# Staggered tracing of projection, MLP and key sums, and LN scaling on ACT, in a kernel of two attention and two MLP layers

## The chip, the cores and the metric

The kernel runs on one core of one Trainium2 chip. The metric is the device time of one execution in microseconds (us), given as the median of several executions. The profiles are single executions. A span is about 2 us shorter than the device time of the same execution (525.43 against 523.7 us for the kernel before). Of the runs e1 to e4 below, a second profile is kept beside the one quoted; between the two, one stretch of the kernel differs by up to 2.7 us. So a difference of one or two us between single profiles is not read as an effect here.

Engine names: PE is TensorE's matmul stream, PEld its weight loads, DVE VectorE, ACT ScalarE, POOL GpSimd, SP the engine that issues most DMAs here. LN is the layer normalization of a tile of rows. The granted clock is the share of TensorE's full clock that it was allowed in a stretch of time.

## The reference, cut to what matters

```python
def _A_ref(x, wqkv, w_phi, wo):          # linear attention, 32 heads of 16
    q, k, v = ...                        # x @ wqkv, split by head
    pq, pk = q @ w_phi, k @ w_phi        # per head
    phi_q = concat(softmax(pq), softmax(-pq))
    phi_k = concat(softmax(pk), softmax(-pk))
    kv = sum over s of phi_k^T v;  z = sum over s of phi_k
    o = (phi_q kv) / (phi_q z + 1e-6)
    return o @ wo

def _B_ref(x, W_gate, W_up, W_down):     # MLP, 512 -> 1376 -> 512
    return (relu(x @ W_gate) * (x @ W_up)) @ W_down

x = x + A(layernorm(x));  x = x + B(layernorm(x))     # x is 2048 x 512, bf16
x = x + A(layernorm(x));  x = x + B(layernorm(x))     # the same weights again
```

An attention layer needs the sums kv and z over all 2048 rows before it can answer the first query. That is a hard joint: all keys of a layer come before its first attention tile. An MLP needs only its own rows.

## The kernel before

The rows are cut into 4 chunks of 512, a chunk into 4 tiles of 128. The residual X stays in SBUF. The query and key weights are folded with `w_phi` once, at the start. LN of a tile makes statistics on DVE, the inverse root on POOL, the scaling on DVE, and a transposing DMA that brings the result into the layout that the matmuls need:

```python
def norm_tile(st, c, ti, dst):
    ...                                                  # bn_stats, bn_aggr -> mv, ve (DVE)
    nc.gpsimd.tensor_tensor(out=rstd[:], in0=ve[:], in1=st.nhalf[:, 0:1], op=Alu.pow)
    xn = st.work.tile([P, D], BF16, name="xn")
    nc.vector.tensor_scalar(out=xn[:], in0=x, scalar1=mv[:, 0:1], scalar2=rstd[:],
                            op0=Alu.subtract, op1=Alu.mult)
    nc.sync.dma_start_transpose(out=dst[:, :, ti * P:(ti + 1) * P], in_=xn[:])
```

A keys tile runs kps (PE), two Exp into ek (ACT), vps (PE), vext (ACT), the sums sk (DVE), phiK = ek / sums (POOL), and kvq (PE), which adds to the sums in PSUM. An attention tile runs erq (PE), rS, Tn, U, dd, o (all DVE), the transposing DMA to oT, yaps (PE) and the addition to X (DVE). An MLP chunk runs gps and ups (PE), rg and ru (ACT), hT (DVE), ybps (PE) and the addition to X (DVE). Keys and MLP have LN at the head of their chunk, and in all three each consumer stands right behind its producer:

```python
    def keys(self, c):
        for ti in range(TPC):
            norm_tile(st, c, ti, xnT)
        for ti in range(TPC):
            ...                              # kps, ek, vps, vext, sk, phiK
            for g in range(G):
                ...                          # kvq of this tile

    def attend(self, c):
        for ti in range(TPC):
            ...                              # erq, rS .. o, transposing DMA o -> oT
            yield 2.6
            ...                              # yaps of this tile, X += yaps
            yield 4

        weave(a.attend(0), AC, seq(a.queries(2), a.queries(3)), 2 * QC)
        weave(a.attend(1), AC, b.mlp(0), BC)     # MLP of chunk 0 beside attention of chunk 1
        weave(a.attend(2), AC, b.mlp(1), BC)
        weave(a.attend(3), AC, b.mlp(2), BC)
```

`weave` only sets the order in which instructions are traced. The order on each engine is fixed when the program is built: what is traced earlier has the higher priority, and something later goes first where the earlier is expected to be still waiting. ("Traced" always means this order of building; a trace of the chip is what the profiler recorded.)

The softmax here doesn't subtract the row's maximum and nothing guards it: scores larger than these inputs give would overflow.

## Time and profile before

| | before |
|---|---|
| device time, median (range) | 525.32 us (522.59 to 527.84) |
| span of the profiled execution | 523.7 us |
| PE busy / idle | 413.3 / 110.4 us |
| mean granted clock of TensorE | 0.922 |

The head of the profile page gives the busy time of each engine, its share of the span and its instructions:

```profile
span 523.7 us, 6113 instructions
...
PE 413.3 (79%) x2103; PEld 197.6 (38%) x2144; DVE 326.4 (62%) x719; ACT 194.3 (37%) x345; POOL 101.9 (19%) x114
```

No engine is full, and PE is the fullest. So the question is what PE waits for. The view of waits has, on each line, who waited for whom, us in total, how often, and the longest:

```profile
PE gps L286 <- DMA xnTB<-xn: 22.9, 7, 5.6
PE kvq L196 <- POOL phiK L188: 18.6, 18, 3.6
PE erq L240 <- DVE Tn L250: 16.1, 8, 2.8
PE erq L240 <- DVE ve L142: 13.2, 4, 3.7
PE yaps L265 <- DMA oT<-o: 11.9, 12, 1.9
```

The first line is the MLP's first matmuls waiting for LN of their chunk, the second the key sums behind phiK, the third and fourth the attention's first matmuls behind DVE, the last the projection behind the transpose of its input. Where this happens is seen in the timeline of PE. Each line has start, duration, what ran, and in brackets the idle time before it and what ended it. This is the joint between MLP 0 and MLP 1 of the first layer:

```profile
139.06 7.30 PE L303 MATMUL ybps<-wd,hT 128*128 128x512 bf16 x32
146.19 0.60 PE L240 MATMUL erq<-R,Eq 128*128 128x144 bf16 x7
148.22 1.04 PE L265 MATMUL yaps<-wo,oT 128*128 128x512 bf16 x4 [1.43 <-DMA oT<-o]
149.09 0.23 PE L240 MATMUL erq<-R,Eq 128*128 128x144 bf16 x1
152.50 1.14 PE L240 MATMUL erq<-R,Eq 128*128 128x144 bf16 x8 [3.18 <-DVE ve L142]
156.26 1.89 PE L286 MATMUL gps<-xnTB,wg 128*128 128x512 bf16 x4 [2.62 <-DMA xnTB<-xn]
```

PE stands still for 1.43 + 3.18 + 2.62 = 7.2 us, and its next group takes 1.89 us where such a group in full stream takes 1.03. The chain of waits over the same joint shows why (start, us, what): everything is in series.

```profile
145.76 2.41 DMA oT<-o
...
148.22 1.05 PE yaps L265 x4
...
149.29 0.69 DVE X_80 L268
...
152.65 0.69 POOL rstd L144
...
153.80 2.41 DMA xnTB<-xn
...
156.26 1.03 PE gps L286 x2
```

The table of windows gives, for a stretch of time, its length and each engine's busy us (with instructions), then the mean granted clock, the DMA share and GB/s. Four stretches matter: first keys phase, first attention start (first erq to first gps), MLP 0 of layer 1, and the second attention start.

```profile
18.90:76.70 57.80, 46.56 (x305) 24.81 (x309) 41.08 (x79) 32.32 (x63) 39.73 (x32) 0.94 0.39 106
76.70:112.20 35.50, 23.27 (x106) 10.41 (x107) 25.66 (x59) 12.90 (x25) 2.19 (x4) 0.80 0.15 30
112.20:156.30 44.10, 36.29 (x178) 17.27 (x182) 27.26 (x63) 13.00 (x22) 2.32 (x4) 0.93 0.12 25
322.50:358.00 35.50, 23.31 (x108) 10.37 (x109) 25.66 (x59) 12.92 (x25) 2.19 (x4) 0.80 0.15 30
```

In the attention starts PE is busy 23 of 35 us and its clock is down to 0.80.

### The profile page before, as it was taken

To read this page: it belongs to the slowest core of one execution; us is meant where nothing else is said; L and a number is where in the kernel's file an instruction comes from. 1 tells how busy PE (TensorE), PEld (TensorE's weight loads), DVE (VectorE), ACT (ScalarE), POOL (GpSimd) and SP (SyncE) were. 2 spreads that over 40 slices of the span, in tenths; PEclk is the share of its full clock that TensorE was granted. 3 is DMA by queue.
4 is the path that set the end of the run, shared out by engine and by line. 5 is a ranking of instruction groups with operands and counts; after the bars stand their busy time and mean duration, and the time that the engine had idled before them with its cause. 6 is when DMAs were issued, how large, how long until landed. Compare 5 with 4: busy or idle time off the path is not lost.

```text
span 523.7 us, 6113 instructions
## 1 busy us (share of the span) xinstructions
PE 413.3 (79%) x2103; PEld 197.6 (38%) x2144; DVE 326.4 (62%) x719; ACT 194.3 (37%) x345; POOL 101.9 (19%) x114
## 2 busy tenths in 40 slices
PE   0678877769949967996977988667994995997697
PEld 0354433324424433442533443323442442343243
DVE  3978636765774677667856773776566467566122
ACT  0545563335205402603655347233600630450260
POOL 3288640000000002004422552000000000000000
PEclk9989997789989997998999999778997999899699
DMA  8538200221011112211310110121112011102001
GB/s 279 122 88 287 32 1 20 41 41 20 11 40 21 22 21 50 41 21 21 61 21 1 21 20 1 30 41 31 21 43 57 12 32 52 40 20 61 10 0 41
DMA packets 59791, 23.53 MB, mean 45 GB/s; under 512 B 52736, under 2 KB 58896, under 8 KB 59760
## 3 DMA queue, kind: packets, MB, share of 16 engines
q1 hardware_dynamic: 56688, 16.79, 14.7%
q0 software_dynamic: 960, 4.24, 2.2%
q10 hardware_dynamic: 2112, 2.10, 1.3%
q8 instruction: 17, 0.28, 0.2%
q14 instruction: 14, 0.11, 0.1%
HBM read 8.44 MB, written 2.10 MB: 20 GB/s over the span
## 4 chain that ended last, share of the span: by engine, by line
PE 52%; DVE 17%; DMA 12%; POOL 9%; issue 6%; ACT 3%; SPq 0%; POOLq 0%; ACTq 0%; DVEq 0%
PE gps L286 13%; PE ups L293 13%; PE ybps L303 9%; POOL phiK L188 7%; DMA oT<-o 6%; PE yaps L265 6%; PE qps L226 4%; DVE sk L184 3%; DVE Tn L250 3%; DMA xnTB<-xn 3%; PE erq L240 2%; DVE bnst L138 2%; DMA X_80<-in_A_x_dram 2%; POOL rstd L144 2%; PE kvq L196 2%
## 5 line engine op out<-in xcount | busy, mean ns | idle before, releaser
L286 PE MATMUL gps<-xnTB,wg 128*128 128x512 bf16 (+1 forms) x347 | 97.0, 404 | 26.6 <-DMA xnTB<-xn 22.9
L289 ACT ACTIVATE rg<-gps 128x512 bf16<-128x512 f32 (+1 forms) x88 | 52.5, 597 | 154.2 <-PE gps L286 144.8
L144 POOL TENSOR_TENSOR rstd<-ve,nhalf 128x1 f32<-128x1 f32 x64 | 35.4, 561 | 334.8 <-DVE ve L142 313.5
L293 PE MATMUL ups<-xnTB,wu 128*128 128x512 bf16 (+1 forms) x342 | 94.1, 395 | 0.6 <-issue 0.2
L297 DVE TENSOR_TENSOR hT<-rg,ru 128x512 bf16<-128x512 bf16 (+1 forms) x88 | 42.3, 482 | 69.5 <-ACT ru L296 69.0
L303 PE MATMUL ybps<-wd,hT 128*128 128x512 bf16 (+1 forms) x342 | 79.5, 379 | 0.5
L188 POOL TENSOR_TENSOR phiK<-ek,sk 128x1024 bf16<-128x1024 bf16 x32 | 61.4, 1926 | 48.2 <-DVE sk L186 45.9
L296 ACT CAST ru<-ups 128x512 bf16<-128x512 f32 (+1 forms) x88 | 51.5, 585 | 36.0 <-PE ups L293 34.5
L286 PEld LDWEIGHTS <-wg 128*128 128x128 bf16 (+1 forms) x352 | 35.9, 104 | 71.0 <-issue 22.9
L293 PEld LDWEIGHTS <-wu 128*128 128x128 bf16 (+1 forms) x352 | 36.7, 105 | 44.1 <-issue 9.1
L184 DVE TENSOR_REDUCE sk<-ek 128x64 f32<-128x1024 bf16 x32 | 38.7, 1212 | 20.2 <-ACT ek L175 20.2
L240 PE MATMUL erq<-R,Eq 128*128 128x144 bf16 x256 | 27.6, 248 | 29.5 <-DVE Tn L250 16.1
L303 PEld LDWEIGHTS <-hT 128*128 128x128 bf16 (+1 forms) x352 | 34.0, 98 | 39.1
L250 DVE TENSOR_TENSOR Tn<-erq,rS 128x816 bf16<-128x816 f32 x64 | 45.8, 716 | 0.8
L265 PE MATMUL yaps<-wo,oT 128*128 128x512 bf16 x124 | 35.7, 410 | 12.4 <-DMA oT<-o 11.9
L226 PE MATMUL qps<-xnTA,Wq_334 128*128 128x512 bf16 x124 | 37.6, 435 | 2.3 <-ACT Eq L229 1.7
L240 PEld LDWEIGHTS <-Eq 128*128 128x128 bf16 x256 | 20.6, 108 | 41.8 <-DVE Tn L250 19.6
L174 ACT ACTIVATE ek<-kps 128x512 bf16<-128x512 f32 x32 | 19.3, 603 | 45.7 <-PE kps L171 42.3
L171 PE MATMUL kps<-Wk_123,xnTA 128*128 128x512 bf16 x124 | 35.4, 389 | 0.5 <-ACT ek L175 0.3
L228 ACT ACTIVATE Eq<-qps 128x512 bf16<-128x512 f32 x32 | 19.1, 598 | 41.9 <-PE qps L226 38.0
L179 PE MATMUL vps<-wv,xnTA 128*128 128x512 bf16 x124 | 34.1, 391 | 0.1
L249 DVE RECIPROCAL rS<-erq 128x48 f32<-128x48 f32 x64 | 22.4, 351 | 14.4 <-PE erq L240 14.4
(68 smaller groups left out, 378.3 us busy)
## 6 DMA issues: line engine op xcount, KB each, us to landing
wg<-in_B_W_gate_dram POOLq DMA_DIRECT2D x1, 1376.0 KB, 6.4
wu<-in_B_W_up_dram POOLq DMA_DIRECT2D x1, 1376.0 KB, 9.1
wd<-in_B_W_down_dram POOLq DMA_DIRECT2D x1, 1280.0 KB, 12.3
wk<-in_A_wqkv_dram ACTq DMA_DIRECT2D x1, 512.0 KB, 4.8
X_79<-in_A_x_dram SPq DMA_DIRECT2D x4, 128.0 KB, 5.7
wv<-in_A_wqkv_dram ACTq DMA_DIRECT2D x1, 512.0 KB, 6.6
wq<-in_A_wqkv_dram ACTq DMA_DIRECT2D x1, 512.0 KB, 8.9
X_80<-in_A_x_dram SPq DMA_DIRECT2D x1, 512.0 KB, 9.4
```

The costliest lines, as they stand in the source:

```text
L144: nc.gpsimd.tensor_tensor(out=rstd[:], in0=ve[:], in1=st.nhalf[:, 0:1], op=Alu.pow)
L184: nc.vector.tensor_reduce(out=sk[:], in_=ek[:].rearrange("p s (h f) -> p (s h) f", f=DH), axis=AX.X, op=Alu.add)
L188: self.mark = nc.gpsimd.tensor_tensor(out=phiK[:].rearrange("p s (h f) -> p (s h) f", f=DH), in0=ek[:].rearrange("p s (h f) -> p (s h) f", ...
L226: nc.tensor.matmul(qps[:], lhsT=st.Wq2[:, m, b * P:(b + 1) * P], rhs=self.xnT[c][:, m, :], start=(m == 0), stop=(m == NDB - 1))
L240: nc.tensor.matmul(kvq[:, bank, slot * ERW:(slot + 1) * ERW], lhsT=Eq[:, b, s, ti * P:(ti + 1) * P], rhs=st.R[:, g, :, :].rearrange("p h c ...
L250: nc.vector.tensor_tensor(out=Tn[:, :, lo:hi, :], in0=Q[:, :, :, 0:DH + 1], in1=rS[:, :, lo:hi].unsqueeze(3).to_broadcast([P, 2, hi - lo, ...
L265: nc.tensor.matmul(yps[:], lhsT=oT[:, b, :], rhs=st.wo[:, b, :], start=(b == 0), stop=(b == NDB - 1))
L286: nc.tensor.matmul(gps[:n, :], lhsT=st.wg[:, b, f * P:f * P + n], rhs=xnT[:, b, :], start=(b == 0), stop=(b == NDB - 1))
L289: nc.scalar.activation(out=rg[:n, :], in_=gps[:n, :], func=AF.Relu)
L293: nc.tensor.matmul(ups[:n, :], lhsT=st.wu[:, b, f * P:f * P + n], rhs=xnT[:, b, :], start=(b == 0), stop=(b == NDB - 1))
L296: nc.scalar.copy(out=ru[:n, :], in_=ups[:n, :])
L303: nc.tensor.matmul(yps[:], lhsT=hT[:n, f, ti * P:(ti + 1) * P], rhs=st.wd[:n, f, :], start=(f == 0), stop=(f == NFT - 1))
```

## The change

The change gives each consumer other work to run in front of it, so that the latency in between is hidden. It has five parts:

1. The MLP of a chunk is traced two attention tiles later than the projection of the chunk's last tile.
2. The projection yaps of a tile is traced behind the attention of the next tile.
3. kvq of a tile (now in `kvz`) is traced behind phiK of the next tile.
4. LN of a tile is traced right behind the residual update that completes it, for the MLP (behind yaps) and for the next layer's keys (behind ybps).
5. The LN scaling moves from DVE to ACT, with the bias -mean x rstd made by a small DVE instruction, nm.

The full diff also moves some queries to other places in the trace, gives xnTB a third buffer and puts the fold's wT into other buffers. No matmul is added or removed. Cut to its core:

```diff
 def norm_tile(st, c, ti, dst):
+    nm = st.small.tile([P, 1], F32, name="nm")
+    nc.vector.scalar_tensor_tensor(out=nm[:], in0=mv[:, 0:1], scalar=-1.0, in1=rstd[:],
+                                   op0=Alu.mult, op1=Alu.mult)
     xn = st.work.tile([P, D], BF16, name="xn")
-    nc.vector.tensor_scalar(out=xn[:], in0=x, scalar1=mv[:, 0:1], scalar2=rstd[:],
-                            op0=Alu.subtract, op1=Alu.mult)
+    nc.scalar.activation(out=xn[:], in_=x, func=AF.Identity, scale=rstd[:], bias=nm[:])
 ...
     def keys(self, c):
-        for ti in range(TPC):
-            norm_tile(st, c, ti, xnT)
+        late = None
         ... (kps to phiK of tile t)
-            (kvq of tile t)
+            if late is not None:
+                self.kvz(*late)
+                yield 2.3
+            late = (t, phiK, vext)
 ...
+    def attends(self, hook):
+        late = None
+        for t in range(self.st.T):
+            oT = self.attend(t)
+            yield 2.3
+            if late is not None:
+                self.project(*late, hook)      # yaps, X += yaps, then hook(c, ti): LN
+                yield 4
+            late = (t, oT)
 ...
-        weave(a.attend(0), AC, seq(a.queries(2), a.queries(3)), 2 * QC)
-        weave(a.attend(1), AC, b.mlp(0), BC)
-        ...
+        at = A.attends(B.norm)
+        weave(take(at, 6 * AT), 6 * AT, seq(*[A.queries(c) for c in range(1 if layer == 0 else 3, NC)]),
+              3 * QC if layer == 0 else QC)
+        weave(take(at, 4 * AT), 4 * AT, B.mlp(0, hook), BC)
+        weave(take(at, 4 * AT), 4 * AT, B.mlp(1, hook), BC)
+        ...
```

More of the change, by code (lines that the diff above doesn't have):

```diff
@@ L102, in fold @@
         dst = const.tile([P, NDB, D], BF16, name=name)
-        wT = st.work.tile([P, NDB, D], BF16, name="wT", bufs=2)
+        wT = st.big.tile([P, NDB, D], BF16, name="wT", tag="hT")
         for m in range(NDB):
@@ L153, in __init__ @@
         self.st = st
-        self.xnT = [None] * st.NC
+        self.xnT = [st.xnt.tile([P, NDB, CH], BF16, name="xnTA", bufs=st.NC) for _ in range(st.NC)]
         self.Eq = [None] * st.NC
@@ L157, in __init__, with norm @@
         self.mark = None
+    def norm(self, c, ti):
+        norm_tile(self.st, c, ti, self.xnT[c])
     def keys(self, c):
@@ L162, in keys @@
             self.kvq = st.ps_q.tile([P, 3, 512], F32, name="kvq", tag="q")
-        self.xnT[c] = xnT = st.xnt.tile([P, NDB, CH], BF16, name="xnTA", bufs=st.NC)
-        for ti in range(TPC):
-            norm_tile(st, c, ti, xnT)
+        xnT = self.xnT[c]
+        late = None
         for ti in range(TPC):
@@ L192, in keys, with kvz @@
             yield 4
-            prev = None
-            for g in range(G):
-                b, s = g // 2, g % 2
-                mm = nc.tensor.matmul(self.kvq[:, g // 3, (g % 3) * GC:(g % 3 + 1) * GC],
-                                      lhsT=phiK[:, s, b * P:(b + 1) * P],
-                                      rhs=vext[:, 8 * b:8 * (b + 1), :].rearrange("p h c -> p (h c)"),
-                                      start=(t == 0 and g % 3 == 0), stop=(t == st.T - 1),
-                                      skip_group_check=True)
-                if t == 0 and prev is not None:
-                    st.tc.keep_in_program_order(mm)
-                prev = mm
-            yield 2.3
+            if late is not None:
+                self.kvz(*late)
+                yield 2.3
+            late = (t, phiK, vext)
+        self.kvz(*late)
+        yield 2.3
+    def kvz(self, t, phiK, vext):
+        st, nc = self.st, self.st.nc
+        for g in range(G):
+            b, s = g // 2, g % 2
+            mm = nc.tensor.matmul(self.kvq[:, g // 3, (g % 3) * GC:(g % 3 + 1) * GC],
+                                  lhsT=phiK[:, s, b * P:(b + 1) * P],
+                                  rhs=vext[:, 8 * b:8 * (b + 1), :].rearrange("p h c -> p (h c)"),
+                                  start=(t == 0 and g % 3 == 0), stop=(t == st.T - 1),
+                                  skip_group_check=True)
+            if t == 0 and g > 0:
+                st.tc.keep_in_program_order(mm)
     def build_R(self):
@@ L230, in queries, with attend @@
             yield 4
-    def attend(self, c):
+    def attend(self, t):
         st, nc = self.st, self.st.nc
+        c, ti = t // TPC, t % TPC
         Eq = self.Eq[c]
-        for ti in range(TPC):
-            kvq = st.ps_q.tile([P, 3, 512], F32, name="erq", tag="q")
-            for g in range(G):
-                b, s = g // 2, g % 2
-                bank, slot = (s, b) if b < 3 else (2, s)
-                nc.tensor.matmul(kvq[:, bank, slot * ERW:(slot + 1) * ERW],
-                                 lhsT=Eq[:, b, s, ti * P:(ti + 1) * P],
-                                 rhs=st.R[:, g, :, :].rearrange("p h c -> p (h c)"),
-                                 start=True, stop=True)
-            rS = st.small.tile([P, 2, H], F32, name="rS")
-            Tn = st.work.tile([P, 2, H, DH + 1], BF16, name="Tn")
-            Q1 = kvq[:, 0:2, 0:3 * ERW].rearrange("p k (h c) -> p k h c", c=DH + 2)
-            Q2 = kvq[:, 2, 0:2 * ERW].rearrange("p (k h c) -> p k h c", k=2, c=DH + 2)
-            for (Q, lo, hi) in ((Q1, 0, 24), (Q2, 24, 32)):
-                nc.vector.reciprocal(out=rS[:, :, lo:hi], in_=Q[:, :, :, DH + 1])
-                nc.vector.tensor_tensor(out=Tn[:, :, lo:hi, :], in0=Q[:, :, :, 0:DH + 1],
-                                        in1=rS[:, :, lo:hi].unsqueeze(3).to_broadcast([P, 2, hi - lo, DH + 1]),
-                                        op=Alu.mult)
-            U = st.work.tile([P, H, DH + 1], BF16, name="U")
-            nc.vector.tensor_tensor(out=U[:], in0=Tn[:, 0, :, :], in1=Tn[:, 1, :, :], op=Alu.add)
-            dd = st.small.tile([P, H], F32, name="dd")
-            nc.vector.reciprocal(out=dd[:], in_=U[:, :, DH])
-            o = st.work.tile([P, D], BF16, name="o")
-            nc.vector.tensor_tensor(out=o[:].rearrange("p (h d) -> p h d", d=DH), in0=U[:, :, 0:DH],
-                                    in1=dd[:].unsqueeze(2).to_broadcast([P, H, DH]), op=Alu.mult)
-            oT = st.work.tile([P, NDB, P], BF16, name="oT")
-            nc.sync.dma_start_transpose(out=oT[:], in_=o[:])
-            yield 2.6
-            yps = st.ps_a.tile([P, D], F32, name="yaps", tag="a")
-            for b in range(NDB):
-                nc.tensor.matmul(yps[:], lhsT=oT[:, b, :], rhs=st.wo[:, b, :],
-                                 start=(b == 0), stop=(b == NDB - 1))
-            x = st.X[c][:, ti, :]
-            nc.vector.tensor_tensor(out=x, in0=x, in1=yps[:], op=Alu.add)
-            yield 4
@@ L272 @@
-class LayerB:
-    def __init__(self, st, last):
-        self.st, self.last = st, last
-    def mlp(self, c):
+        kvq = st.ps_q.tile([P, 3, 512], F32, name="erq", tag="q")
+        for g in range(G):
+            b, s = g // 2, g % 2
+            bank, slot = (s, b) if b < 3 else (2, s)
+            nc.tensor.matmul(kvq[:, bank, slot * ERW:(slot + 1) * ERW],
+                             lhsT=Eq[:, b, s, ti * P:(ti + 1) * P],
+                             rhs=st.R[:, g, :, :].rearrange("p h c -> p (h c)"),
+                             start=True, stop=True)
@@ new lines, in attend @@
+        rS = st.small.tile([P, 2, H], F32, name="rS")
+        Tn = st.work.tile([P, 2, H, DH + 1], BF16, name="Tn")
+        Q1 = kvq[:, 0:2, 0:3 * ERW].rearrange("p k (h c) -> p k h c", c=DH + 2)
+        Q2 = kvq[:, 2, 0:2 * ERW].rearrange("p (k h c) -> p k h c", k=2, c=DH + 2)
+        for (Q, lo, hi) in ((Q1, 0, 24), (Q2, 24, 32)):
+            nc.vector.reciprocal(out=rS[:, :, lo:hi], in_=Q[:, :, :, DH + 1])
+            nc.vector.tensor_tensor(out=Tn[:, :, lo:hi, :], in0=Q[:, :, :, 0:DH + 1],
+                                    in1=rS[:, :, lo:hi].unsqueeze(3).to_broadcast([P, 2, hi - lo, DH + 1]),
+                                    op=Alu.mult)
@@ new lines, in attend @@
+        U = st.work.tile([P, H, DH + 1], BF16, name="U")
+        nc.vector.tensor_tensor(out=U[:], in0=Tn[:, 0, :, :], in1=Tn[:, 1, :, :], op=Alu.add)
+        dd = st.small.tile([P, H], F32, name="dd")
+        nc.vector.reciprocal(out=dd[:], in_=U[:, :, DH])
+        o = st.work.tile([P, D], BF16, name="o")
+        nc.vector.tensor_tensor(out=o[:].rearrange("p (h d) -> p h d", d=DH), in0=U[:, :, 0:DH],
+                                in1=dd[:].unsqueeze(2).to_broadcast([P, H, DH]), op=Alu.mult)
@@ new lines, in attend, with project @@
+        oT = st.work.tile([P, NDB, P], BF16, name="oT")
+        nc.sync.dma_start_transpose(out=oT[:], in_=o[:])
+        return oT
+    def project(self, t, oT, hook):
+        st, nc = self.st, self.st.nc
+        c, ti = t // TPC, t % TPC
+        yps = st.ps_a.tile([P, D], F32, name="yaps", tag="a")
+        for b in range(NDB):
+            nc.tensor.matmul(yps[:], lhsT=oT[:, b, :], rhs=st.wo[:, b, :],
+                             start=(b == 0), stop=(b == NDB - 1))
+        x = st.X[c][:, ti, :]
+        nc.vector.tensor_tensor(out=x, in0=x, in1=yps[:], op=Alu.add)
+        hook(c, ti)
@@ new lines, in attends, with __init__, norm, mlp @@
+    def attends(self, hook):
+        late = None
+        for t in range(self.st.T):
+            oT = self.attend(t)
+            yield 2.3
+            if late is not None:
+                self.project(*late, hook)
+                yield 4
+            late = (t, oT)
+        self.project(*late, hook)
+        yield 4
+class LayerB:
+    def __init__(self, st):
+        self.st = st
+        self.xnT = {}
+    def norm(self, c, ti):
+        if ti == 0:
+            self.xnT[c] = self.st.xnt.tile([P, NDB, CH], BF16, name="xnTB", bufs=3)
+        norm_tile(self.st, c, ti, self.xnT[c])
+    def mlp(self, c, hook):
@@ L277, in mlp @@
         st, nc = self.st, self.st.nc
-        xnT = st.xnt.tile([P, NDB, CH], BF16, name="xnTB")
-        for ti in range(TPC):
-            norm_tile(st, c, ti, xnT)
+        xnT = self.xnT[c]
         hT = st.big.tile([P, NFT, CH], BF16, name="hT")
@@ L306, in mlp @@
             nc.vector.tensor_tensor(out=x, in0=x, in1=yps[:], op=Alu.add)
-            if self.last:
-                nc.sync.dma_start(out=st.ov[:, c * TPC + ti, :], in_=x)
+            hook(c, ti)
             yield 11
@@ L314, in seq, with take, weave @@
         yield from g
-def run(gen):
-    for _ in gen:
-        pass
-def weave(main, main_cost, fill, fill_cost):
-    done_m = done_f = 0.0
-    live_m = live_f = True
-    while live_m or live_f:
-        if live_m and (not live_f or done_m / main_cost <= done_f / fill_cost):
-            try:
-                done_m += next(main)
-            except StopIteration:
-                live_m = False
-        else:
-            try:
-                done_f += next(fill)
-            except StopIteration:
-                live_f = False
-KC, QC, AC, BC = 41.2, 16.0, 26.4, 132.0
+def take(gen, cost):
+    done = 0.0
+    while done < cost:
+        n = next(gen, None)
+        if n is None:
+            return
+        yield n
+        done += n
+def weave(a, cost_a, b, cost_b):
+    gens, costs, done = [a, b], [cost_a, cost_b], [0.0, 0.0]
+    while gens[0] is not None or gens[1] is not None:
+        i = 0 if gens[1] is None or (gens[0] is not None and done[0] / costs[0] <= done[1] / costs[1]) else 1
+        n = next(gens[i], None)
+        if n is None:
+            gens[i] = None
+        else:
+            done[i] += n
+KC, QC, AT, BC = 41.2, 16.0, 6.3, 132.0
+GU = 88.0
 @with_exitstack
@@ L345, with store @@
     st = setup(ctx, tc, A_x, A_wqkv, A_w_phi, A_wo, B_W_gate, B_W_up, B_W_down, out)
-    NC = st.NC
+    nc, NC = st.nc, st.NC
     assert NC == 4
-    A1, B1, A2, B2 = LayerA(st), LayerB(st, False), LayerA(st), LayerB(st, True)
-    run(A1.keys(0))
-    st.load_B(A1.mark)
-    st.Wq2 = st.fold_q()
-    run(A1.keys(1))
-    run(A1.keys(2))
-    run(A1.keys(3))
-    for (a, b, nxt) in ((A1, B1, A2), (A2, B2, None)):
-        run(a.queries(0))
-        run(a.queries(1))
-        a.build_R()
-        weave(a.attend(0), AC, seq(a.queries(2), a.queries(3)), 2 * QC)
-        weave(a.attend(1), AC, b.mlp(0), BC)
-        weave(a.attend(2), AC, b.mlp(1), BC)
-        weave(a.attend(3), AC, b.mlp(2), BC)
-        if nxt is not None:
-            weave(seq(nxt.keys(0), nxt.keys(1), nxt.keys(2)), 3 * KC, b.mlp(3), BC)
-            run(nxt.keys(3))
-        else:
-            run(b.mlp(3))
+    def store(c, ti):
+        nc.sync.dma_start(out=st.ov[:, c * TPC + ti, :], in_=st.X[c][:, ti, :])
+    A = LayerA(st)
+    for c in range(NC):
+        for ti in range(TPC):
+            A.norm(c, ti)
+        weave(A.keys(c), KC, iter(()), 1.0)
+        if c == 0:
+            st.load_B(A.mark)
+            st.Wq2 = st.fold_q()
+    weave(A.queries(0), QC, iter(()), 1.0)
+    for layer in range(2):
+        B = LayerB(st)
+        N = LayerA(st) if layer == 0 else None
+        hook = N.norm if N is not None else store
+        A.build_R()
+        at = A.attends(B.norm)
[3 more added lines that the diff above has]
+        weave(take(at, 4 * AT), 4 * AT, B.mlp(1, hook), BC)
+        if N is None:
+            weave(at, 2 * AT, B.mlp(2, hook), BC)
+            weave(B.mlp(3, hook), BC, iter(()), 1.0)
+        else:
+            weave(seq(at, N.keys(0)), 2 * AT + KC, B.mlp(2, hook), BC)
+            b3 = B.mlp(3, hook)
+            weave(seq(N.keys(1), N.keys(2)), 2 * KC, take(b3, GU + 22), GU + 22)
+            weave(N.queries(0), QC, b3, 22)
+            weave(seq(N.queries(1), N.queries(2)), 2 * QC, N.keys(3), KC)
+        A = N
 _INS = ['A_x', 'A_wqkv', 'A_w_phi', 'A_wo', 'B_x', 'B_W_gate', 'B_W_up', 'B_W_down']
```

## The prediction

> **What bounds the kernel now.** TensorE: 413 us busy of 523.7 (the page's first part); DVE 326, ACT 194. Where it streams, four 128x512 matmuls start every 0.86 us (timeline of PE). At that pace my estimate for all matmuls is 373 us: 1,568 of 512 columns x 0.216, 512 short ones x about 0.06, the folds. So about 150 us are lost: 110 idle, 40 run slowly. It is slow just after a gap: an MLP's first gps group took 1.89 us instead of 1.03, and the granted clock was 0.80 and 0.79 in the two attention starts (table of windows). The Trainium skill ("TensorE: Matmul & The Clock Gate", Part 1) says that idleness throttles the clock; this trace agrees.
>
> The idle time lies at the joints (timeline of PE):
> - start, 16 us
> - first keys phase, 10 us behind phiK on POOL; keys beside MLP 3, 5; keys 3, 4
> - the attention starts, 76.7 to 112.2 and 323 to 358: PE busy 23 of 35 us
> - each MLP boundary: oT transpose, erq, last LN, xnTB transpose (2.4 us each to land) in series. 146.8 to 156.3 has 7.2 us of gaps, then about 2 us of slow clock. With six such boundaries: 50 to 60 us.
>
> **What the change does.** No matmul is removed.
> 1. MLP two attention tiles later: its xnTB is ready before its matmuls are due. Removes most boundary gaps.
> 2. Projection one tile later: the next erq goes ahead of yaps, hiding the oT transpose. kvq one tile later hides phiK (1.93 us on POOL).
> 3. LN behind each residual update, also for the next layer's keys: transposes fall into the MLP.
> 4. xn leaves DVE (64 x 0.45 = 29 us); nm adds 64 x about 0.16 = 10. DVE falls to about 308. ACT gets 64 x about 0.79 us (0.60 of the trace's ACTIVATE plus two pointer operands at 93 ns, "ScalarE: Activation LUTs", What ACT_TABLE_LOAD costs; no run here shows that yet) = 50 us, to about 245. It has room.
>
> **What stays.** The start (19 us). Attention starts stay DVE-bound: a tile costs DVE 3.6 (rS to o) + 0.68 (X) + about 1.3 (LN) = 5.6 us, five tiles before the first MLP can go: about 32 us, in layer 2 with only 3.5 us of queries as filler. In layer 1's MLPs 0 and 1 DVE then needs 4 x 5.6 + 11 x 0.48 + 4 x 0.68 + 4 x 1.3 = 36 us against PE's 34: nearly equal, so I take 38.5 each.
>
> **Sum by stage (before -> after).** Start 19 -> 19. Keys to first erq 58 -> 52. Attention start 35.5 -> 32. MLP 0, 1, 2: 133 -> 38.5 + 38.5 + 42 = 119 (the last with keys 0). MLP 3 with keys, queries: 57 + 21 -> 52 + 17. Attention start 35 -> 32. MLP 0, 1, 2: 131 -> 36 + 35 + 33 = 104. MLP 3 and tail 34.7 -> 32. Total 459 us.
>
> **Prediction: 459 us**, 436 to 484 at 8 in 10. Faster by over 2%: 0.96; within 2%: 0.03; slower: 0.01.
>
> **What would show it.** PE idle from 110 to about 55 us; gps waiting for xnTB from 22.9 to under 6; kvq behind phiK from 18.6 to under 6; mean clock from 0.92 to about 0.95; DVE near 308, ACT near 245; both attention starts still 30 us or more with the low clock.
>
> **What would make it wrong.** DVE works in order: hT or the ybps update queued behind an attention chain would hold MLP stages at 42 us (towards 484). Or MLP 0 overlaps the attention start, which shrinks (towards 436).

## The result, and the profile after

| | before | after |
|---|---|---|
| device time, median (range) | 525.32 (522.59 to 527.84) | 473.86 (472.66 to 475.46) |
| ratio to before, 95% interval | 1 | 0.9023 (0.897 to 0.9076) |
| PE busy / idle | 413.3 / 110.4 | 397.7 / 74.8 |
| mean granted clock | 0.922 | 0.952 |

A ratio is the mean time of one kernel's fast runs over the mean of the other's fast runs of the same rounds, so it is not quite the ratio of the medians.

The time is inside the predicted range, 15 us above the point. The head of the page after:

```profile
span 472.5 us, 6159 instructions
...
PE 397.7 (84%) x2104; PEld 195.2 (41%) x2144; DVE 307.4 (65%) x719; ACT 236.7 (50%) x409; POOL 102.7 (22%) x114
```

DVE lost 19 us and ACT gained 42. The waits of PE after:

```profile
PE erq L250 <- DVE Tn L260: 20.2, 9, 4.1
PE kvq L208 <- POOL phiK L192: 15.8, 13, 2.0
...
PE yaps L279 <- DMA oT<-o: 6.2, 6, 2.4
PE kps L175 <- DMA xnTA<-xn: 5.1, 2, 4.9
PE gps L316 <- DMA xnTB<-xn: 1.8, 1, 1.8
```

gps waits for LN went from 22.9 to 1.8 us and yaps for oT from 11.9 to 6.2. But kvq still waits 15.8 us behind phiK. And kps waits 5 us for LN of the first layer's own keys, a wait that was not among those of before. The same joint between MLP 0 and MLP 1, in the timeline of PE:

```profile
149.76 2.54 PE L333 MATMUL ybps<-wd,hT 128*128 128x512 bf16 x11
152.13 0.66 PE L250 MATMUL erq<-R,Eq 128*128 128x144 bf16 x8
152.63 1.03 PE L316 MATMUL gps<-xnTB,wg 128*128 128x512 bf16 x4
153.50 1.03 PE L323 MATMUL ups<-xnTB,wu 128*128 128x512 bf16 x4
```

There is no bracket, so no gap, and gps takes 1.03 us at once. The windows of the same four stretches after:

```profile
18.30:81.40 63.10, 46.11 (x304) 23.78 (x308) 37.80 (x77) 40.44 (x76) 38.33 (x29) 0.97 0.35 98
81.40:116.90 35.50, 25.41 (x120) 12.17 (x122) 27.99 (x68) 15.28 (x27) 2.65 (x5) 0.76 0.18 36
116.90:152.60 35.70, 35.29 (x190) 17.40 (x192) 30.43 (x80) 18.87 (x31) 3.56 (x7) 1.00 0.21 43
303.90:338.90 35.00, 17.60 (x87) 8.49 (x90) 29.44 (x70) 6.39 (x10) 2.19 (x4) 0.70 0.23 38
```

MLP 0 fell from 44.1 to 35.7 us, with PE busy 35.3 of them at full clock. The first keys phase grew from 57.8 to 63.1 us, with PE busy the same 46 us. The attention starts did not change in length.

All stretches together, cut at first matmuls of the groups named, read from the timelines of PE:

| stretch | before | predicted | after |
|---|---|---|---|
| start, to the first kps | 18.9 | 19 | 18.3 |
| keys, to the first erq | 57.8 | 52 | 63.1 |
| attention start 1, to the first gps | 35.5 | 32 | 35.5 |
| MLP 0, 1, 2 of layer 1 | 133 | 119 | 113.9 |
| MLP 3, keys, to the next erq | 77 | 69 | 73.1 |
| attention start 2 | 35.5 | 32 | 35.0 |
| MLP 0, 1, 2 of layer 2 | 131 | 104 | 101.2 |
| MLP 3 and end | 35 | 32 | 32.4 |
| sum | 523.7 | 459 | 472.5 |

Four things are to be explained: the keys phase that got longer (11 us above the prediction), the stretch of MLP 3 (4 above), the attention starts (3.5 and 3 above), and which parts of the change earned the 51 us.

### The profile page after: what moved, and what is told of

It reads as the page before. It is cut to its first block, busy times and chain, and to the rows that moved or that the text cites. A ratio compares the mean times of both kernels' runs of the same rounds, so it can differ in the third digit from the quotient of the medians.

```text
span 472.5 us, 6159 instructions
## 1 busy us (share of the span) xinstructions
PE 397.7 (84%) x2104; PEld 195.2 (41%) x2144; DVE 307.4 (65%) x719; ACT 236.7 (50%) x409; POOL 102.7 (22%) x114
## 4 chain that ended last, share of the span: by engine, by line
PE 43%; DVE 6%; POOL 3%; issue 2%; DMA 2%; ACT 2%; SPq 0%; POOLq 0%; ACTq 0%
PE gps L316 11%; PE ups L323 11%; PE ybps L333 11%; PE yaps L279 3%; PE kps L175 2%; POOL phiK L192 2%; PE vps L183 2%; PE erq L250 2%; PE kvq L208 1%; DVE Tn L260 1%; DMA xnTB<-xn 1%; DMA oT<-o 1%; DVE sk L188 1%; POOL rstd L144 1%; DVE bnst L138 1%
## 5 line engine op out<-in xcount | busy, mean ns | idle before, releaser
L316 PE MATMUL gps<-xnTB,wg 128*128 128x512 bf16 (+1 forms) x348 | 91.1, 381 | 3.3 <-DMA xnTB<-xn 1.8
L323 PE MATMUL ups<-xnTB,wu 128*128 128x512 bf16 (+1 forms) x343 | 89.5, 379 | 1.4 <-ACT rg L319 0.7
L192 POOL TENSOR_TENSOR phiK<-ek,sk 128x1024 bf16<-128x1024 bf16 x32 | 61.8, 1934 | 64.0 <-DVE sk L190 32.9
L327 DVE TENSOR_TENSOR hT<-rg,ru 128x512 bf16<-128x512 bf16 (+1 forms) x88 | 40.6, 462 | 45.3 <-ACT ru L326 45.1
L323 PEld LDWEIGHTS <-wu 128*128 128x128 bf16 (+1 forms) x352 | 34.8, 100 | 39.7 <-issue 2.0
L250 PE MATMUL erq<-R,Eq 128*128 128x144 bf16 x256 | 25.2, 246 | 21.7 <-DVE Tn L260 20.2
L279 PE MATMUL yaps<-wo,oT 128*128 128x512 bf16 x125 | 37.9, 431 | 6.2 <-DMA oT<-o 6.2
L175 PE MATMUL kps<-Wk_123,xnTA 128*128 128x512 bf16 x122 | 34.2, 393 | 5.3 <-DMA xnTA<-xn 5.1
L236 PE MATMUL qps<-xnTA,Wq_345 128*128 128x512 bf16 x121 | 36.6, 427 | 2.0 <-ACT Eq L239 1.2
L208 PEld LDWEIGHTS <-phiK 128*128 128x128 bf16 x256 | 16.2, 98 | 24.4 <-POOL phiK L192 21.0
```

The costliest lines, as they stand in the source:

```text
L175: nc.tensor.matmul(kps[:], lhsT=xnT[:, b, ts], rhs=st.Wk2[:, b, :], start=(b == 0), stop=(b == NDB - 1))
L192: self.mark = nc.gpsimd.tensor_tensor(out=phiK[:].rearrange("p s (h f) -> p (s h) f", f=DH), in0=ek[:].rearrange("p s (h f) -> p (s h) f", ...
L250: nc.tensor.matmul(kvq[:, bank, slot * ERW:(slot + 1) * ERW], lhsT=Eq[:, b, s, ti * P:(ti + 1) * P], rhs=st.R[:, g, :, :].rearrange("p h c ...
L279: nc.tensor.matmul(yps[:], lhsT=oT[:, b, :], rhs=st.wo[:, b, :], start=(b == 0), stop=(b == NDB - 1))
L316: nc.tensor.matmul(gps[:n, :], lhsT=st.wg[:, b, f * P:f * P + n], rhs=xnT[:, b, :], start=(b == 0), stop=(b == NDB - 1))
L323: nc.tensor.matmul(ups[:n, :], lhsT=st.wu[:, b, f * P:f * P + n], rhs=xnT[:, b, :], start=(b == 0), stop=(b == NDB - 1))
```

## The experiments

Each was compared with the kernel before, run in the same rounds on the same chip. They were run in four batches on four chips, where the kernel before had medians of 523.6 to 525.8 us, so a difference between two medians of different batches is good to about 2 us. "Stretch" is one of the table above.

| run | edit | median us | ratio to before (95%) |
|---|---|---|---|
| after | | 473.86 | 0.9023 (0.897 to 0.9076) |
| e1_xn_on_dve | after, LN scaling on DVE | 465.16 | 0.8854 (0.8818 to 0.889) |
| e2_load_late | after, MLP weights loaded later | 475.25 | 0.9061 (0.9006 to 0.9116) |
| e3_mlp_no_lag | after, no MLP lag | 494.24 | 0.9394 (0.9348 to 0.944) |
| e4_proj_now | after, no projection lag | 493.48 | 0.9409 (0.9362 to 0.9456) |
| e5_kvz_now | after, no kvq lag | 490.13 | 0.9351 (0.9286 to 0.9416) |
| e6_ln_late | after, next layer's LN at the head of keys | 480.76 | 0.9158 (0.9106 to 0.9211) |
| e7_before_xn_act | before, LN scaling on ACT | 533.52 | 1.016 (1.011 to 1.0211) |
| e8_o_on_pool | e1, o on POOL | 466.62 | 0.8879 (0.8836 to 0.8923) |
| e9_queries_first | e1, queries traced ahead of attention | 469.94 | 0.8969 (0.894 to 0.8998) |
| e10_first_ln_on_dve | after, only the first keys' LN scaling on DVE | 467.91 | 0.892 (0.8867 to 0.8973) |
| e11_half_phik | e1, half of phiK left out (wrong result) | 462.62 | 0.8823 (0.8784 to 0.8862) |
| e12_no_den | e1, last division left out (wrong result) | 455.54 | 0.8669 (0.8608 to 0.873) |

### LN scaling back on DVE

```diff
-    nc.scalar.activation(out=xn[:], in_=x, func=AF.Identity, scale=rstd[:], bias=nm[:])   # and nm
+    nc.vector.tensor_scalar(out=xn[:], in0=x, scalar1=mv[:, 0:1], scalar2=rstd[:],
+                            op0=Alu.subtract, op1=Alu.mult)
```

> The kernel after, with the LN scaling back on DVE as before (xn one DVE instruction, nm gone); everything else of the change kept. Theory A (the scaling on ACT is a real part of the gain because DVE is nearly as loaded as PE in layer 1's MLP stages: 30.4 us of 35.7 in MLP 0): DVE gets about 18 us more work net, MLP 0 and 1 of layer 1 lengthen by 1 to 3 us each, total 478 to 484 us. Rival B (the gain is all from the re-ordering; the move to ACT is neutral or costs time, because in the first keys phase [...]its xn stand behind the Exp and the casts): the stretch from the first kps to the first erq falls from 62.8 to under 58 us, MLP stages stay within 1 us, total 466 to 474 us.

465.16 us, correct, and faster than the kernel after; the two intervals do not overlap. Theory A falls. Theory B holds for the keys stretch, which is 57.0 us (57.2 in the second profile); the total is just below its range, because the rest moved too: MLP 0 to 3 with the keys of layer 1 took 183.4 us (in both profiles) instead of 187.0, the attention starts 33.8 each (35.5 and 33.9 in the second profile), and only layer 2's MLPs and the end grew, by 1.7 us. The window of the keys stretch of this run:

```profile
18.50:75.50 57.00, 44.69 (x310) 23.28 (x308) 40.92 (x79) 31.97 (x63) 39.71 (x32) 1.00 0.39 107
```

The waits of DVE for ACT inside this stretch are in three lines, one for each kernel: before, after, this run.

```profile
DVE sk L184 <- ACT ek L175: 8.5, 9, 1.8
```

```profile
DVE sk L188 <- ACT ek L179: 19.0, 12, 5.7
```

```profile
DVE sk L186 <- ACT ek L177: 7.8, 8, 1.8
```

With xn on ACT, DVE's reduce of the Exp waits 11 us more for ACT. DVE is spared 3 us of busy time in the stretch (40.9 to 37.8) and stands idle for much more. This is the lowest median of the correct kernels; e8 and e10 are not clear of it, since their intervals overlap with its own.

### The same move alone, in the kernel before

```diff
-    nc.vector.tensor_scalar(out=xn[:], ...)
+    (nm on DVE)
+    nc.scalar.activation(out=xn[:], in_=x, func=AF.Identity, scale=rstd[:], bias=nm[:])
```

> The kernel before, with one part of the change alone: LN scaling on ACT with nm on DVE. From the run that put it back on DVE (465 against 474 us, first keys stretch 57.0 against 63.1): Theory A (in the first keys phase ACT is in the chain and pays for it in any order of tracing): first keys stretch grows from 57.8 to 61 us or more, total 526 to 533. Rival B (the move costs only in the new order of tracing; here ACT has 194 us of 524 and the LN of a chunk stands at its head): first keys stretch within 1.5 us of 57.8, total 518 to 526.

533.52 us: slower than before by 1.1 to 2.1%, an interval that reaches across the 2% line, so the formal verdict is "unclear" though it excludes no change. Theory A holds (the total is 0.5 us above its range). The window and the wait of the first keys stretch of this run:

```profile
18.20:81.50 63.30, 46.38 (x306) 23.97 (x309) 37.88 (x78) 40.67 (x76) 38.41 (x30) 0.97 0.35 98
```

```profile
DVE sk L186 <- ACT ek L177: 19.0, 12, 5.6
```

They are those of the kernel after, nearly to the digit. So the longer keys stretch is the work of this part of the change alone, in either order of tracing. All profiles agree: the ten with the first keys' scaling on ACT have a keys stretch of 61.8 to 66.1 us, the eight with it on DVE 56.6 to 57.9. Over the whole kernel the move costs about 8 us here and 8.7 in the new order. Here only 5.5 of that is the first keys stretch: from the first gps to the next layer's first erq it took 216.3 us against 210.3, and the two attention starts gave 3.8 back.

### ACT scaling everywhere but in the first keys phase

```diff
     for c in range(NC):
         for ti in range(TPC):
-            A.norm(c, ti)
+            norm_tile(st, c, ti, A.xnT[c], on_act=False)
```

> The kernel after, with LN scaling on DVE only for the 16 tiles of the first keys phase; the other 48 stay on ACT. Theory A (the move costs in the first keys phase, where ACT's Exp and casts stand in one queue with xn, and gains or is neutral elsewhere): first keys stretch 57 to 58 us, total 464 to 469, equal to or better than all on DVE (465). Rival B (it costs everywhere, as the layer-1 MLP stretch of 183.4 against 187.0 us suggests): first keys stretch 57 to 58, but the rest as in the kernel after, total 467 to 471.

467.91 us, the keys stretch 57.2. That settles the keys stretch once more. For the remaining 48 tiles the answer leans to B: MLP 0 to 3 with the keys took 187.9 us and attention start 2 took 35.0, as in the kernel after (187.0 and 35.0). But the intervals of this run and of the one with all scaling on DVE overlap, so outside the first keys phase I can only say that no gain from ACT is seen.

### Weight loads out of the way

```diff
         if c == 0:
-            st.load_B(A.mark)
             st.Wq2 = st.fold_q()
+        if c == 2:
+            st.load_B(A.mark)
```

> The kernel after, with the MLP weights' loads issued after the phiK of keys chunk 2 instead of chunk 0; nothing else moved. In the kernel after, PE stands still for 4.9 us at 43.3 us waiting for an xnTA transpose, while the weight loads are in flight, and the stretch from the first kps to the first erq took 62.8 us where I had predicted 52. Theory A (the weight loads hold the LN transposes up): that gap goes, the stretch falls by 4 to 8 us, total 466 to 470 us. Rival B (the stretch is bound by the chain kps, Exp, DVE reduce, POOL phiK and by xn on ACT; the gap only moves): stretch within 2 us of 62.8, total 472 to 476 us.

475.25 us: no change. Theory A falls, theory B holds. The 4.9 us gap before kps disappeared from the timeline, but the stretch stayed long (66.1 us in the second profile), and so did the wait of DVE for ACT:

```profile
18.10:82.60 64.50, 47.49 (x314) 26.05 (x312) 39.19 (x77) 43.37 (x80) 38.25 (x30) 0.93 0.34 96
```

```profile
DVE sk L188 <- ACT ek L179: 17.9, 8, 9.2
```

The largest visible gap of the stretch was not its cause; when it went, others took its place.

### No MLP lag

```diff
-        weave(take(at, 6 * AT), 6 * AT, seq(queries ...), ...)
+        weave(take(at, 4 * AT), 4 * AT, seq(queries ...), ...)
 ...
-            weave(at, 2 * AT, B.mlp(2, hook), BC)            # likewise in layer 1
+            weave(at, 4 * AT, B.mlp(2, hook), BC)
```

> The kernel after, with each MLP chunk traced right behind the projection of its fourth attention tile (four tiles taken instead of six before the first MLP, four left beside the third); all else kept. Theory A (the lag of two tiles is what removes the boundary waits): gps waits for xnTB again, 10 to 20 us in total, and total 485 to 505 us. Rival B (the late projection, and LN right behind the residual, already do it, since the scheduler orders by priority and readiness): gps wait under 6 us, total 470 to 478 us.

494.24 us: the lag is worth 20 us, and theory A holds. The waits at the joints came back. Theory A expected 10 to 20 us of gps behind xnTB; 4.8 us stand under that name, and the rest under two that I had not listed, LN's DVE instructions. The three add up to 15.5 us.

```profile
PE gps L316 <- DVE nm L146: 5.7, 1, 5.7
...
PE gps L316 <- DVE ve L142: 5.0, 1, 5.0
```

### No projection lag

```diff
         for t in range(self.st.T):
             oT = self.attend(t)
             yield 2.3
-            if late is not None:
-                self.project(*late, hook)
-                yield 4
-            late = (t, oT)
+            self.project(t, oT, hook)
+            yield 4
```

> The kernel after, with each attention tile's projection traced right behind its own attention again (no lag of one tile); MLP lag, LN and kvz kept. Theory A (the lag hides the oT transpose of 2.4 us and its PE stop): PE waits for oT grow from 6.2 us to 15 or more, attention starts lengthen by 2 to 5 us each, total 480 to 490 us. Rival B (with an MLP tracing two tiles later PE has other work to do meanwhile, and at the attention starts DVE is the limit): total 470 to 477 us.

493.48 us, 20 us more; the size is above what theory A expected, the wait as it expected:

```profile
PE yaps L279 <- DMA oT<-o: 21.1, 22, 2.3
```

The place is another one than A said: the attention starts did not lengthen (34.6 and 30.7 us); MLP 0 to 3 with the keys grew to 195.0 and layer 2 from its first gps on from 129.9 to 144.9. Traced right behind its attention, a projection stops PE in the middle of an MLP: 18 of the 22 waits come after a layer's first gps. So both lags are needed, each against waits inside the MLP stages.

### No kvq lag

```diff
-            if late is not None:
-                self.kvz(*late)
-                yield 2.3
-            late = (t, phiK, vext)
+            self.kvz(t, phiK, vext)
+            yield 2.3
```

> The kernel after, with each tile's kvq accumulation traced right behind its phiK again (no lag of one tile); all else kept. Theory A (the lag hides phiK's 1.93 us on POOL, as I predicted): kvq's waits behind phiK grow from 15.8 us to 20 or more, total 477 to 483 us. Rival B (the scheduler orders PE by readiness in either case and phiK comes late because ACT and DVE are late, so the lag does nothing; kvq still waited 15.8 us in the kernel after against 18.6 before): waits and total unchanged within 2 us, 472 to 476.

490.13 us, 16 us more, where theory A allowed 3 to 9. The wait doubled:

```profile
PE kvq L203 <- POOL phiK L191: 30.9, 23, 2.9
```

Again the place is telling. The first keys stretch is no longer than in the kernel after (61.8 against 63.1), and kvq's waits in it are the same with and without the lag (11.1 and 11.2 us; 10.1 in the kernel before). All the loss lies where keys run beside MLP 2 and MLP 3: from the first gps to the next layer's first erq 204.7 us instead of 187.0.

### Next layer's LN at the head of its keys

```diff
-        hook = N.norm if N is not None else store
+        hook = (nothing) if N is not None else store
+        (keys(c) of layer 2 begins with LN of its 4 tiles)
```

> The kernel after, with the LN of the second attention layer taken off the MLP's residual update and done at the head of each keys chunk again (as before); LN of the MLP's input stays behind the attention's residual. Theory A (the early LN spares the keys phase beside MLP 3 its LN and transposes): the stretch from the first MLP to the second layer's first erq (187 us in the kernel after) grows by 4 to 10 us, total 478 to 484. Rival B (those LNs load ACT and DVE in MLP 0 and 1 of layer 1 for nothing, PE has other work while the keys' LN runs): stretch within 2 us of 187, total 471 to 475.

480.76 us, and the stretch 192.1: theory A holds. Early LN of the next layer is worth 7 us. The wait that came back is one of 7.0 us, that of layer 2's first keys for their LN; the rest of the line is the first layer's:

```profile
PE kps L179 <- DMA xnTA<-xn: 11.2, 2, 7.0
```

### Is the first keys phase bound by phiK on POOL?

```diff
-                out=phiK[:], in0=ek[:], in1=sk[:] broadcast     (all 1024 columns)
+                out=phiK[:, 0, :], in0=ek[:, 0, :], in1=sk[:, 0:H] broadcast
 ...
-                lhsT=phiK[:, s, ...]
+                lhsT=(phiK if s == 0 else ek)[:, s, ...]
```

> Wrong result on purpose. The kernel after with LN scaling on DVE, and phiK's multiply on POOL done for half of the columns only (about 1.0 us instead of 1.93); kvq reads the unscaled Exp for the other half (ek has a fourth buffer for it). Theory A (the first keys stretch of 57 us, PE busy 46, is bound by POOL's phiK in its chain, so that the one-tile lag of kvq hides nothing there): stretch falls by 5 us or more, to 52 or less. Rival B (it is bound by DVE's reduce, reciprocal and LN, 3.5 us a tile, and by their order): stretch within 2 us of 57.

462.62 us, with a wrong result. phiK's mean fell to 1.06 us and POOL's work in the stretch by 14 us:

```profile
18.40:75.00 56.60, 46.89 (x302) 24.63 (x306) 39.66 (x79) 31.45 (x62) 25.89 (x32) 0.94 0.40 108
```

The stretch is 56.6 us against 57.0: theory A falls. The granted clock was lower here (0.94 against 1.00) and PE's work 2.2 us longer, which can hide a gain of about 2 us, but not the 5 us that A needs. This fits a lag that hides phiK and does nothing there. What does bound the stretch stays open: rival B names DVE's work and its order, but no run here took DVE's reduce away, and PE, busy 46.9 of the 56.6 us, is busier than DVE. The medians of this run and its base are 2.5 us apart, with intervals that overlap; in the profiles the time saved is elsewhere: from the end of MLP 2 of layer 1 to the next erq it took 70.5 us where its base took 73.3. In the kernel after, the gaps of kvq behind phiK in that stretch add up to 1.25 + 1.49 + 0.49 + 1.47 = 4.7 us.

### What holds the attention starts: three runs

First, DVE relieved of o by POOL:

```diff
-        nc.vector.tensor_tensor(out=o[:] ..., in0=U[:, :, 0:DH], in1=dd[:] ..., op=Alu.mult)
+        nc.gpsimd.tensor_tensor(out=o[:] ..., in0=U[:, :, 0:DH], in1=dd[:] ..., op=Alu.mult)
```

> The kernel after with LN scaling on DVE, and the last multiply of each attention tile (o, 0.68 us on DVE) on POOL, where I estimate 0.97 us from phiK's 1.93 us for twice the elements. Theory A (the attention starts are bound by DVE's own work of 5.6 us a tile, as I predicted): five tiles save 3 us, both attention starts shrink from 33.8 to 31 or less, total 457 to 461. Rival B (they are bound by the chain erq, DVE, oT, yaps at TensorE's low clock and by the frozen order of TensorE's instructions; DVE idles there): attention starts within 1 us of 33.8, or longer because rstd waits behind o on POOL, total 464 to 470.

466.62 us. o took 1.10 us on POOL. The starts were 36.2 and 32.4 us, together 68.6, where the base had 67.6 in one profile and 69.4 in the other: no shorter, though DVE's work fell. First the windows of the base, e1, then those of this run:

```profile
75.50:109.40 33.90, 22.89 (x124) 10.60 (x122) 29.12 (x67) 12.09 (x23) 2.20 (x4) 0.90 0.19 39
292.80:326.60 33.80, 17.58 (x89) 8.52 (x90) 28.33 (x65) 3.26 (x6) 2.20 (x4) 0.71 0.19 38
```

```profile
75.60:111.90 36.30, 24.87 (x121) 11.48 (x122) 25.92 (x61) 12.17 (x23) 8.39 (x10) 0.81 0.18 37
297.60:329.90 32.30, 17.43 (x86) 8.96 (x89) 23.64 (x57) 3.26 (x6) 8.43 (x10) 0.68 0.21 41
```

DVE's sum of work alone is not the bound, against theory A as I had put it.

Second, the queries traced ahead of the attention:

```diff
-    weave(A.queries(0), QC, iter(()), 1.0)
+    for c in range(NC):
+        weave(A.queries(c), QC, iter(()), 1.0)
 ... (and the fourth chunk's queries of layer 2 behind its keys)
```

> The kernel after with LN scaling on DVE, and all four chunks' queries traced before the attention starts (none beside its first tiles). In that base the two attention starts took 33.8 us each with DVE busy about 29 us, 6 to 7 attention tiles worked on, and TensorE at a low clock running query groups between an erq and the yaps. Theory A (DVE-bound by 6 to 7 tiles' work, whatever TensorE does beside): attention starts stay at 32 to 35 us, the queries' TensorE time appears elsewhere, total 466 to 474. Rival B (query groups at the low clock stand in front of erq and yaps and hold DVE up): attention starts fall to 30 us or less and the total stays within 3 us of 465.

469.94 us. In the first start the edit failed: the trace has 45 query matmuls in it, as many as in the base; I take it that they fill PE while the last key sums are awaited and after, wherever they are traced. It says nothing there. In the second start the count went from 12 to 0, and the start took 33.3 us against 33.8:

```profile
300.60:333.90 33.30, 15.38 (x76) 8.03 (x78) 27.21 (x63) 0.00 (x0) 2.19 (x4) 0.58 0.19 38
```

TensorE's query work does not hold that start up; rival B falls there. As a whole this run is 4.8 us slower than its base, with intervals that do not overlap. Its first start took 37.2 us and MLP 0 to 3 with the keys 187.1 (33.8 and 183.4 in the base); why was not looked into.

Third, the last division of each attention tile left out, which shortens both DVE's work and the chain from erq to oT:

```diff
-        U = Tn[0] + Tn[1];  dd = 1 / U[:, :, DH];  o = U * dd
+        o = Tn[0] + Tn[1]
```

> Wrong result on purpose. The kernel after with LN scaling on DVE, and the last division of each attention tile left out: dd (0.35 us) and o (0.68 us) go, U becomes the 512-column add straight into o. So DVE loses about 1.0 us of 5.6 a tile, and the chain from erq to oT is shorter by as much; with o on POOL DVE had lost 0.68 us too, but the chain had become longer, and the two attention starts had not shrunk (36.2 and 32.4 against 33.8 and 33.8). Theory A (the attention starts are bound by the work and chain of 6 to 7 tiles on DVE): each falls by 4 to 7 us, to 27 to 30. Rival B (they are bound by TensorE's order and low clock, the oT and xnTB transposes and rstd on POOL): each falls by less than 2 us.

455.54 us, with a wrong result. The starts:

```profile
76.50:105.90 29.40, 21.23 (x123) 10.59 (x125) 24.51 (x57) 13.03 (x25) 2.74 (x5) 0.94 0.23 45
291.50:321.90 30.40, 16.65 (x86) 9.19 (x88) 22.93 (x54) 3.26 (x6) 2.19 (x4) 0.72 0.23 44
```

They fell by 4.4 and 3.4 us: the first just inside theory A's range, the second just below it, both clearly more than rival B allows. Taking work off DVE helps where the chain gets shorter with it. I read the starts as bound by DVE's chain of 6 to 7 tiles for most of their length; that only half to two thirds of the 1.0 us a tile came back shows that it is not the whole. The second start is the cleaner of the two: its clock is that of the base (0.72 against 0.71), while the first start's was higher (0.94 against 0.90).

## Why the prediction was right or wrong, point by point

**The signs that I had listed.** Met: the mean clock (0.952, about 0.95 expected), DVE (307 us, 308), gps behind xnTB (1.8 us, under 6), and the two attention starts (35 us at a low clock, 30 or more). ACT came out at 237 us, not 245. Missed: PE idle (74.8 us, about 55 expected) and kvq behind phiK (15.8 us, under 6).

**The boundaries: right.** gps waiting for xnTB: predicted under 6 us, measured 1.8. The MLP stages: predicted 119 and 104 us, measured 113.9 and 101.2. Undoing the MLP lag costs 20 us, undoing the projection lag 20, each shown alone.

**"kvq one tile later hides phiK": half right.** I had predicted under 6 us of waits in total and a shorter first keys phase; 15.8 us remained. The lag works beside the MLP (16 us, more than I had counted for it) and does nothing in the first keys phase. There, phiK can even be halved and the stretch changes by 0.4 us.

**"xn leaves DVE ... It has room": the step that failed.** The costs were right: DVE 307 us (308 predicted), xn on ACT 0.82 us on average (0.79 predicted) against 0.45 on DVE, nm 0.18. The conclusion was wrong. I added up busy times and took the spare share of ACT over the whole kernel for spare time in the keys phase. But there ACT's Exp feeds DVE's reduce. xn put 13 more instructions into ACT's list inside this stretch (76 against 63), of 0.82 us each, and DVE then waited 19.0 instead of about 8 us for the Exp. Predicted: the stretch falls from 58 to 52 us. Measured: 63.1; with the scaling on DVE 57.0; and in the kernel before, the move alone gives 63.3. So a term that I had entered as a gain was a loss of about 6 us, and of 8.7 us in the whole kernel (473.86 against 465.16). The other 5 us by which the stretch missed its 52 are the gain from hiding phiK that did not come. The Trainium skill, "ScalarE: Activation LUTs", Rules for kernel authors, advises VectorE for plain multiplies and adds; this agrees, with 0.45 against 0.82 us for the same tile. How exactly the 6 us arise (xn standing ahead of Exp in ACT's list, or LN that comes late) was not separated. The longest of DVE's waits in the kernel after, 5.7 us, is of the second kind: just before it, kps (4.9 us) and ACT's own next xn (5.1 us) both wait for the transposing DMA into xnTA. But the run with late weight loads removed that gap and the stretch stayed long.

**Attention starts: by the sums, a shift and not a loss.** I had counted five tiles before the first MLP and 32 us. The chip worked on 6 to 7 tiles there (the trace counts 6 to 7 of each of U, dd and o) and took 35 us. Those tiles were then missing from the MLPs' load, which came out shorter by nearly as much: attention start plus three MLPs was predicted at 151 and 136 us and measured at 149.4 and 136.2. That the two errors (6.5 us up, 7.9 us down) nearly cancel in the total was not foreseen. The low clock there stayed, as predicted (0.76 and 0.70).

**MLP 3 with keys: 4 us too little.** The gaps of kvq behind phiK, 4.7 us there, are the term that I had taken to be hidden. Halving phiK gave 2.8 of them back.

**The sum.** Keys phase 11.1 above, MLP 3 stretch 4.1 above, all the rest together 1.7 below: 13.5 us, which is the difference of 472.5 and 459.

**Where the 51 us came from**, by undoing one part at a time: MLP lag 20, projection lag 20, kvq lag 16, early LN of the next layer 7, scaling on ACT minus 9. The sum is 54 against 51.5 measured. That does not show that the parts add up: LN behind the attention's residual, the new places of the queries and the buffers were not undone, and are in none of these.

## What to carry to other kernels

When a consumer waits for a latency (a transposing DMA, another engine), let the trace put one or two tiles of other work between them; here this cost no instruction and each such lag was worth 16 to 20 us. Before moving work to an engine with a low busy share, look at the stage where that engine is in the chain of waits, and test that move alone: in the kernel before, DVE got 18 us lighter by it and the kernel about 8 us slower. And do not take the largest gap of a stretch for its cause until removing it has made the stretch shorter.

## What the Trainium skill lacked or had wrong

- "TensorE: Matmul & The Clock Gate", Back-to-back issue gap, gives about 131 ns per matmul of 512 columns for a sustained stream with weight loads. In the kernel after, MLP 2 of layer 2 streams its 44 ybps (43 of them recorded) from 430.62 to the next group at 440.13 us, 216 ns each, which is the figure that this section calls the isolated one. The page contradicts itself here: its Part 1 gives 215.7 ns for back-to-back matmuls of this size, and this agrees with that.
- The same page, Part 3 (The mechanism), says that weight loads overlap running matmuls only when the row group differs. In MLP 0 of the kernel after, nearly all loads are of 128 rows; PEld is busy 17.4 us of 35.7 while PE is busy 35.3, so they overlap. The same section's sentence on a background weight buffer, as a second way to load early, would fit; no run here tests it.
- "DMA: Bandwidth & Descriptors", DMA Transpose, has no latency of a small transpose within SBUF. It took 2.4 us from issue to landing for a 128x512 bf16 tile, the median of each of the three groups of 32 (xnTA, oT, xnTB) in both kernels, and it is the largest single piece of the chain at the joints.
- No page that I read warns that an engine's free share of the whole span says nothing of a stage. Here ACT at 37% was no free place in the keys phase: moving the scalings of 0.82 us there lengthened it by 5.5 us in one kernel (57.8 to 63.3) and 6.1 in the other (57.0 to 63.1).
